# Eighteen chunks of softmax weights: computed on VectorE beside the attention, or left to ACT

## The chip, the cores and the metric

The kernel runs on one core of a Trainium2 chip. The metric is device time in microseconds (us) from the first to the last instruction of the core. Before the change it is 982.9 us, the median of three runs (981.16 to 983.02). The profile that is read below belongs to the run of 983.02 us; by its own records the span is 981.3 us, with a mean granted TensorE clock of 0.993 of full speed.

## The reference, cut to what matters

```python
# q: 4 x 12288 x 128, kv: 4 x 384 x 32 x 128, w_sr: 128 x 128
kv_pool = kv.reshape(B, H // 4, 4, W // 4, 4, C).mean(axis=(2, 4))   # 4 x 768 x 128
k = v = kv_pool.reshape(B, -1, C) @ w_sr
s = (q @ k.transpose(0, 2, 1)) / sqrt(128)
a = exp(s - max);  a /= a.sum(-1)
x = a @ v                                  # 49152 tokens x 128
h = x @ w_in                               # 49152 x 2048
g = h * sigmoid(1.702 * h)
out = g @ w_out                            # 49152 x 128
```

So there is an attention with 768 keys for each batch of queries, and behind it a feed-forward layer with a gate ("MoE" in the names, but with one expert).

## The kernel before

The tokens are cut into 96 groups of 512 (`NG`), four groups to a supergroup (24 of them, `NS`). The program runs twice through "attention, then feed-forward", each time for 12 supergroups. Within an attention the 768 keys of a group are six chunks of 128 keys (`JC`); a feed-forward has 16 chunks of 128 hidden features for each group.

A *fill* is a matmul with 512 columns into a bank of PSUM; three banks make a *unit*, and ACT turns a unit into weights with one instruction of 128x1536 (exponential in the attention, the gate function in the feed-forward). TensorE also works off the weights (*drain*): a feed-forward chunk with one matmul of 512 columns, an attention chunk with four matmuls of 129 columns, for which the text says "AV".

```python
def fill_attn(chunks, ps):
    for k, (i, jc) in enumerate(chunks):
        rhs = qTs[i // 4][:, 0, (i % 4) * G:(i % 4 + 1) * G]
        nc.tensor.matmul(ps[:, k, :], kTs[i // GB][:, jc * 128:(jc + 1) * 128], rhs,
                         start=True, stop=True)
    nc.scalar.activation(place([("a",) + c for c in chunks]), ps, AF.Exp, scale=scale)
```

`place` takes a free place in the ring `ag`, which has 102 places for chunks. A host loop at the end of the program decides in which order the instructions are emitted; it keeps a model of the time (`now` for TensorE in units of one matmul of 512 columns, `end` for ACT, `dve` for VectorE). The order on each engine is then fixed: an instruction that has to wait makes all later ones of its engine wait too.

```python
    FIXED, CHUNK, SWITCH, HANDOVER, EVACUATE, LATE = 0.295, 1.978, 6.0, 1.0, 4.5, 1.0
    ...
    SMALL, TURN = 0.26, 5.5
```

Some chunks of weights are made by VectorE instead of ACT. One matmul (line 391) fills a bank, and `early_exp` computes the exponential with ten instructions on 128x512:

```python
    def early_exp(ps, out):
        ...
        nc.vector.tensor_scalar(a, ps, scale / LN2, -126.0, MUL, MAX)
        nc.vector.tensor_scalar(b, a, 127.0, MAGIC, MIN, ADD)
        nc.vector.tensor_scalar(e, b, MAGIC - 127.0, 2.0 ** 23, SUB, MUL)
        nc.vector.scalar_tensor_tensor(b, b, MAGIC, a, SUB, SUB)
        nc.vector.tensor_scalar_mul(a, b, COEFFS[5])
        for k in (4, 3, 2, 1):
            nc.vector.scalar_tensor_tensor(a, a, COEFFS[k], b, ADD, MUL)
        nc.vector.scalar_tensor_tensor(out, a, COEFFS[0], e.bitcast(F32), ADD, MUL)
```

There are two kinds of them. Twenty-four (`early`: groups 48 to 51, all six chunks) are made during the first feed-forward, for the attention that follows. Eighteen (`rolling`) are made within the two attentions: the last chunk of the last group of a supergroup, for supergroups 5 to 11 and 13 to 23.

```python
    rolling = [(4 * s + 3, JC - 1) for s in range(NS) if 4 * s > early[-1] or QS < s < XS]
    aside = agpool.tile([128, K, 512], BF, name="aside")
    ...
    def early_fits(p, i, jc):
        if (i, jc) in rolling:
            group = ...                      # the group whose unit was filled last
            return (i // GB, jc) in vs and i // 4 - 1 <= group // 4 and len(used) > rolling.index((i, jc)) - K
        return low and min(slot_of.values()) >= low and (2, JC - 1) in vs

    def early_waits(t):                      # a tile's AV holds back until the model says the chunk is made
        return any(made.get((t // 4, jc), 1e9 if (t // 4, jc) in early_todo else 0.0) > now for jc in range(JC))
```

So the chunk of supergroup s is begun when the fills have come to supergroup s - 1. Its queries are in the tile `qT` of supergroup s, which is loaded by a transposing DMA that is issued two supergroups ahead:

```python
    def background(i):                       # called when group i is filled for the first time
        s = i // 4
        if i % 4 == 0:
            if QS <= s + 2 < NS:
                load_qT(s + 2)               # SyncE: transposing DMA from q_bf
            if CAST <= s + CAST < NS:
                gate()
                cast_q(s + CAST)             # GpSimd: q to bf16, DRAM to DRAM
        if i == 10:
            gate()
            for jc in range(JC):
                load_chunk(1, jc)            # GpSimd: keys of batch 1
```

Of the kernel before, what the change touches and what calls it, by code (L numbers as in the profile page):

```python
# [7 lines left out]
F32 = mybir.dt.float32  # L8
F32R = mybir.dt.float32r
I32 = mybir.dt.int32  # L10
BF = mybir.dt.bfloat16
# [13 lines left out]
def kernel(  # L25
    ctx, tc, q, kv, w_sr, moe_w_in, moe_w_out, out,
):
    nc = tc.nc
    B, N, C = q.shape
# [4 lines left out]
    JC = J // 128  # L34
# [5 lines left out]
    NG = B * N // G  # L40
    NS = NG // 4
    GB = NG // B
    SB = NS // B
    K = 3
    T = 128
    TS = 3
# [12 lines left out]
    R = 2  # L59
    XS = NS // R  # L60
# [3 lines left out]
    cpool = ctx.enter_context(tc.tile_pool(name="const", bufs=1))  # L64
# [5 lines left out]
    agpool = ctx.enter_context(tc.tile_pool(name="ag", bufs=1))  # L70
    npool = ctx.enter_context(tc.tile_pool(name="norm", bufs=3))
# [7 lines left out]
    banks = ppool.tile([128, 8, 512], F32, name="banks")  # L79
# [33 lines left out]
    kv_tiles, kv_sums, pooled, pTs, kTs, vs = {}, {}, {}, {}, {}, {}  # L113
# [32 lines left out]
    def value_chunk(b, jc):  # L146
        ps = acc()
        nc.tensor.matmul(ps[:, 0:128], pTs.pop((b, jc)), w_sr_sb, start=True, stop=True)
        nc.vector.tensor_copy(vs[b][:, jc, 0:C], ps[:, 0:128])
        vs[b, jc] = True  # L150

    def key_and_value(b, jc):
        if jc == 0:
            new_keys(b)
        ps = acc()
        nc.tensor.matmul(ps[:, 0:128], w_sr_sb, pTs[b, jc], start=True, stop=True)
        nc.tensor.matmul(ps[:, 128:256], pTs.pop((b, jc)), w_sr_sb, start=True, stop=True)
        nc.vector.tensor_copy(kTs[b][:, jc * 128:jc * 128 + 128], ps[:, 0:128])
        nc.vector.tensor_copy(vs[b][:, jc, 0:C], ps[:, 128:256])
        vs[b, jc] = True  # L160


    def add_kv(b, n):
# [26 lines left out]
    def make_v(b, a):  # L190
        ps = acc()
        pT = pTs.pop((b, a))
        for k in range(K):
            nc.tensor.matmul(ps[:, k * C:(k + 1) * C], pT[:, k * 128:(k + 1) * 128], w_sr_sb,
                             start=True, stop=True)
        nc.vector.tensor_copy(vs[b][:, a * K:(a + 1) * K, 0:C], ps[:, :h].rearrange("p (k c) -> p k c", k=K))
        for jc in range(a * K, a * K + K):
            vs[b, jc] = True

    qTs = {}  # L200

# [10 lines left out]
    QS = 4  # L212
# [19 lines left out]
        else:  # L232
            nc.vector.tensor_copy(dst, src)  # L233

    w_sr_f = npool.tile([128, 512], F32, name="ea", bufs=1)[:, 0:C]
    nc.sync.dma_start(out=w_sr_f, in_=w_sr)
    load_q(0, 0, 1)
    load_chunk(0, 0)
# [9 lines left out]
    ones = cpool.tile([128, 32], BF)  # L248
# [10 lines left out]
    for m in range(0, 128, 32):  # L259
        p = slice(m, m + 32)  # L260
# [17 lines left out]
    w_out_sb = cpool.tile([128, FCH, C], BF)  # L278

    ag = agpool.tile([128, AG, 512], BF, name="ag")  # L280
    wide = cpool.tile([128, 128], F32R)
    nc.vector.tensor_copy(wide.rearrange("p (a b) -> p a b", b=32), ones.unsqueeze(1).broadcast_to([128, 4, 32]))

    def warm_wide(n):
        for _ in range(n):
            nc.tensor.matmul(banks[:, 2, :], wide, wide.unsqueeze(1).broadcast_to([128, 4, 128]), start=True, stop=True)

    warm(8)
    transpose_q(0)
# [4 lines left out]
    slot_of = {}  # L294
    low = 0
# [26 lines left out]
        return K * len(free_frames())  # L322

    early = range(NG // R, NG // R + EARLY)
    rolling = [(4 * s + 3, JC - 1) for s in range(NS) if 4 * s > early[-1] or QS < s < XS]
    aside = agpool.tile([128, K, 512], BF, name="aside")

    def weights(c):
        if c[0] == "a" and c[1] in early:
            return ag[:, (c[1] - early[0]) * JC + c[2], :]  # L330
        if c[0] == "a" and c[1:] in rolling:
            return aside[:, rolling.index(c[1:]) % K, :]
        return ag[:, slot_of[c], :]


# [9 lines left out]
    def drain_attn(t, a):  # L345

        i, u, k = t // 4, t // TS, t % TS
        if k == a == 0:
            av_of[u] = acc(("av", u))
        o = t % 4 * T  # L350
        for jc in range(a * K, a * K + K):
            nc.tensor.matmul(av_of[u][:, k * (C + 1):(k + 1) * (C + 1)], weights(("a", i, jc))[:, o:o + T],  # L352
                             vs[i // GB][:, jc, 0:C + 1], start=(jc == 0), stop=(jc == JC - 1))
            if t % 4 == 3 and (i, jc) in rolling:
                used.append((i, jc))
            elif t % 4 == 3 and i not in early:
                del slot_of["a", i, jc]
        if k == TS - 1 and a == 1:
            close(("av", u), max(now, dve - 1.0) + EVACUATE)
            on_dve(4.3)  # L360
            ps = av_of.pop(u)[:, 0:TS * (C + 1)].rearrange("p (k c) -> p k c", k=TS)
            rec = npool.tile([128, TS], F32, name="rec")
            nc.vector.reciprocal(rec, ps[:, :, C])  # L363
            n, o = divmod(u * TS, RT)
            if o >= LATER[n]:
                to = x[:, o * T:(o + TS) * T].rearrange("p (k c) -> p k c", k=TS)
            else:
                if u % 2 == 0:
                    xt_of[u // 2] = npool.tile([128, 2 * TS, C], BF, name="xt")
                to = xt_of[u // 2][:, u % 2 * TS:u % 2 * TS + TS, :]  # L370
            nc.vector.tensor_tensor(to, ps[:, :, 0:C], rec.unsqueeze(2).broadcast_to([128, TS, C]), MUL)  # L371
            if u % 2 and o < LATER[n]:
                turns.append((now + TURN, u // 2))
            if n and (o + TS) % PART == 0:
                m = o // PART
                put_away(n, m)
                if m:
                    bring_back(n, m - 1)
                if m == RT // PART - 1:
                    bring_back(n, m)  # L380
# [14 lines left out]
    def early_step():  # L395
        nonlocal steps
        on_dve(next(steps))
        if steps.gi_frame.f_locals["last"]:
            steps = None
            made[early_todo.pop(0)] = dve  # L400

    def early_exp(ps, out):
        last = False
# [17 lines left out]
        last = True  # L421
        yield 3.5

    made, used = {}, []
    steps, early_todo = None, [c for c in rolling if c[0] < early[0]]
    early_todo += [(i, jc) for i in early for jc in range(JC)]
    early_todo += [c for c in rolling if c[0] > early[-1]]

    def early_fits(p, i, jc):
        if (i, jc) in rolling:  # L430
            group = seq[p][1][0][0] if seq[p][0] == "a" else seq[p][1][0][0] // (NG // R) * (NG // R) + NG // R - 1
            return (i // GB, jc) in vs and i // 4 - 1 <= group // 4 and len(used) > rolling.index((i, jc)) - K
        return low and min(slot_of.values()) >= low and (2, JC - 1) in vs

    def early_waits(t):
        return any(made.get((t // 4, jc), 1e9 if (t // 4, jc) in early_todo else 0.0) > now for jc in range(JC))

    def turn(w):

# [116 lines left out]
    chunks, sizes = [], [1, 3, 3, 1, 3, 1, 3, 1] + [3, 3, 2] * 4  # L556
    chunks += [(i, jc) for jc in range(2) for i in range(4)]
    chunks += [(i, jc) for jc in range(2) for i in range(4, 8)]
    chunks += [(i, jc) for jc in range(2, JC) for i in range(8)]
    chunks += [(i, jc) for i in range(8, NG) for jc in range(JC) if i not in early and (i, jc) not in rolling]  # L560
    seq, todo = [], []
    todo_early = [("a", t, a) for t in range(NT) for a in range(2) if (t // TS * TS + TS - 1) // 4 in early]
    for n in range(R):
# [12 lines left out]
    at = {}  # L576
# [3 lines left out]
    for i in early:  # L580
        for jc in range(JC):
            at["a", i, jc] = at["a", early[-1] + 1, 0] - 1
    for i, jc in rolling:
        at["a", i, jc] = at["a", i, 0]
    for kind, t, a in [k for k in todo + todo_early if k[0] == "a"]:
        at["at", t, a] = max(at["a", t // 4, jc] for jc in range(a * K, a * K + K))

# [46 lines left out]
    now, end, extra_at = 0.0, [], 0.0  # L634
    source, dve = None, 0.0
# [25 lines left out]
    for n in range(len(seq)):  # L661
        fill(n + 2)
        while True:
            room = room_ahead()
            limit = end[-1] - K - HANDOVER if n + 3 < len(seq) else 1e9
            bank = free[next_acc()]
            f = None
            if turns and max(now, bank) >= turns[0][0]:
                f, args = turn, turns[0][1:]
            if f is None and extras and now >= max(extra_at, bank):  # L670
                f, *args = extras[0]
            if steps and dve <= now + 2.0:
                early_step()
            if not f and not steps and early_todo and early_fits(min(n + 2, len(seq) - 1), *early_todo[0]) and dve <= now + 2.0 and now >= bank:
                f, args = early_fill, early_todo[0]
            if f and max(now, bank) + COST[f][0] > limit + (LATE if f is turn else 0.0 if f is early_fill else 4.5) and room >= 4 * K:
                f = None
            if f:
                now = max(now, bank) + COST[f][0]
# [11 lines left out]
                continue  # L691
            if not source:

                if todo_early and not any(early_waits(t) for t in range(todo_early[0][1], todo_early[0][1] + TS)):
                    source = todo_early
                else:
                    source = todo
            if not source:
                break
            kind, i, c = source[0]  # L700
            needs = at[("at" if kind == "a" else kind, i, c)]
            cost = K * SMALL if kind == "a" else 1.0
            first_of = c == 0 and (kind == "m" or i % TS == 0)
            if source is not todo_early and (needs > n or (kind == "a" and first_of and at["at", i + TS - 1, 1] > n)
                                             or (kind == "a" and (early_waits(i) or first_of and early_waits(i + TS - 1)))):
                if first_of:
                    source = None
                break
# [47 lines left out]
```

The softmax here doesn't subtract the row's maximum and nothing guards it: scores larger than these inputs give would overflow.

## Time and profile before

| engine | busy us | share of the span | what it does |
|---|---|---|---|
| PE (TensorE) | 953.1 | 97% | fills, drains, transposes |
| ACT | 936.9 | 95% | 512 gate units, 183 exponential instructions |
| DVE (VectorE) | 444.5 | 45% | 42 chunks of weights, evacuations, transposes of the output |
| POOL (GpSimd) | 65.7 | 7% | casting and accumulating DMAs |
| DMA | | mean 91 GB/s | 89.67 MB |

TensorE and ACT are both busy nearly all the time, so the places to look at are those where one of them is not. The page's second part gives the busy share of each engine in 40 slices of the span, 24.5 us each: in the third slice (49 to 74 us) PE and ACT both have the digit 6, between digits of 8 and 9, and the clock row has an 8. The order of the program: loads and first groups until about 40 us, first attention until 153 us, first feed-forward until about 505 us, second attention until 620 us, second feed-forward to the end.

### The profile page before, as it was taken

To read this page: it belongs to the slowest core of one execution; us is meant where nothing else is said; L and a number is where in the kernel's file an instruction comes from. 1 tells how busy PE (TensorE), PEld (TensorE's weight loads), DVE (VectorE), ACT (ScalarE), POOL (GpSimd) and SP (SyncE) were. 2 spreads that over 40 slices of the span, in tenths; PEclk is the share of its full clock that TensorE was granted. 3 is DMA by queue.
4 is the path that set the end of the run, shared out by engine and by line. 5 is a ranking of instruction groups with operands and counts; after the bars stand their busy time and mean duration, and the time that the engine had idled before them with its cause. 6 is when DMAs were issued, how large, how long until landed. Compare 5 with 4: busy or idle time off the path is not lost.

```text
span 981.3 us, 15454 instructions
## 1 busy us (share of the span) xinstructions
PE 953.1 (97%) x6359; PEld 508.6 (52%) x6359; DVE 444.5 (45%) x914; ACT 936.9 (95%) x700; POOL 65.7 (7%) x113
## 2 busy tenths in 40 slices
PE   7869999999999999999999999999999999999997
PEld 3546777744444444454445777664444444444443
DVE  4437767601477778777636677661101101101101
ACT  4969999999899999999999999999999999999995
POOL 3100100330000132000000000000000000000000
PEclk9989999999999999999999999999999999999999
DMA  9894752799772499324438776326222222222223
GB/s 182 164 194 87 118 99 45 108 150 172 160 141 33 77 150 137 45 33 77 64 57 137 162 140 147 91 65 125 37 43 42 34 43 42 36 42 43 34 42 53
DMA packets 354165, 89.67 MB, mean 91 GB/s; under 512 B 328048, under 2 KB 351728, under 8 KB 353776
## 3 DMA queue, kind: packets, MB, share of 16 engines
q1 hardware_dynamic: 323936, 56.06, 32.5%
q0 software_dynamic: 29104, 32.51, 21.7%
q8 instruction: 49, 0.80, 0.3%
q10 hardware_dynamic: 1056, 0.13, 0.1%
q14 instruction: 20, 0.16, 0.1%
HBM read 52.49 MB, written 45.88 MB: 100 GB/s over the span
## 4 chain that ended last, share of the span: by engine, by line
PE 82%; ACT 13%; DMA 3%; DVE 1%; issue 0%; POOL 0%; POOLq 0%
PE banks L540 34%; PE banks L533 32%; ACT ag L343 9%; PE banks L352 7%; PE banks L341 7%; ACT ag L535 3%; DMA qT<-q_bf 2%; PE banks L391 1%; DMA x<-in_q_dram 1%; DVE qT L233 1%; PE banks L444 0%; DVE xt L371 0%; PE banks L227 0%; PE banks L134 0%; DVE x L446 0%
## 5 line engine op out<-in xcount | busy, mean ns | idle before, releaser
L535 ACT ACTIVATE ag<-banks 128x1536 bf16<-128x1536 f32 x512 | 689.6, 1519 | 6.4 <-PE banks L533 6.2
L533 PE MATMUL banks<-x,w_in_sb 128*128 128x512 bf16 x1536 | 415.0, 379 | 4.0 <-ACT ag L535 3.0
L540 PE MATMUL banks<-ag,w_out_sb 128*128 128x512 bf16 x1536 | 410.2, 379 | 0.0
L343 ACT ACTIVATE ag<-banks 128x1536 bf16<-128x1536 f32 (+1 forms) x183 | 241.5, 1496 | 22.0 <-PE banks L341 21.9
L540 PEld LDWEIGHTS <-w_out_sb 128*128 128x128 bf16 x1536 | 149.9, 98 | 179.2 <-issue 0.2
L533 PEld LDWEIGHTS <-w_in_sb 128*128 128x128 bf16 x1536 | 147.9, 98 | 172.8 <-issue 6.9
L548 DVE STREAM_TRANSPOSE o_sb<-banks 128x512 f32<-128x512 f32 x96 | 68.8, 716 | 360.0 <-PE banks L540 344.3
L352 PEld LDWEIGHTS <-ag 128*128 128x128 bf16 x2232 | 145.6, 98 | 45.7 <-issue 1.0
L352 PE MATMUL banks<-v,ag 128*128 128x129 bf16 x2232 | 164.1, 221 | 0.4 <-DVE xt L371 0.2
L341 PE MATMUL banks<-qT,kT 128*128 128x512 bf16 x534 | 146.5, 382 | 5.6 <-ACT ag L343 4.5
L418 DVE SCALAR_TENSOR_TENSOR ea<-ea,eb 128x512 f32<-128x512 f32 x168 | 115.2, 686 | 3.8
L341 PEld LDWEIGHTS <-kT 128*128 128x128 bf16 x534 | 47.0, 98 | 35.4 <-issue 5.1
L371 DVE TENSOR_TENSOR x<-banks,rec 128x384 bf16<-128x384 f32 x104 | 58.0, 558 | 3.6
L407 DVE TENSOR_SCALAR ea<-banks 128x512 f32<-128x512 f32 x42 | 29.1, 692 | 60.1 <-PE banks L391 59.9
L363 DVE RECIPROCAL rec<-banks 128x3 f32<-128x3 f32 x128 | 22.9, 179 | 55.2 <-PE banks L352 54.9
L168 POOL DMA_DIRECT2D kvs<-in_kv_dram x32 | 40.5, 1299 | 33.5 <-DMA kvs<-in_kv_dram 31.1
L469 POOL MEMSET gate_tile<- 1x8 f32 x38 | 3.9, 101 | 450.8 <-DVE gate_tile L468 450.7
L413 DVE SCALAR_TENSOR_TENSOR eb<-eb,ea 128x512 f32<-128x512 f32 x42 | 28.9, 689 | 1.0
L391 PE MATMUL banks<-qT,kT 128*128 128x512 bf16 x42 | 16.1, 384 | 9.1 <-DMA qT<-q_bf 9.1
L415 DVE TENSOR_SCALAR ea<-eb 128x512 f32<-128x512 f32 x42 | 18.2, 434 | 0.9
L411 DVE TENSOR_SCALAR ee<-eb 128x512 int32<-128x512 f32 x42 | 17.9, 427 | 1.3
L409 DVE TENSOR_SCALAR eb<-ea 128x512 f32<-128x512 f32 x42 | 17.8, 423 | 1.0
(68 smaller groups left out, 199.9 us busy)
## 6 DMA issues: line engine op xcount, KB each, us to landing
out_dram<-o_sb SPq DMA_DIRECT2D x382, 64.0 KB, 2.0
kvs<-in_kv_dram POOLq DMA_DIRECT2D x32, 384.0 KB, 6.5
q_bf<-in_q_dram POOLq DMA_DIRECT2D x20, 512.0 KB, 5.8
x_bf<-x SPq DMA_DIRECT2D x13, 768.0 KB, 5.7
x<-in_kv_dram POOLq DMA_DIRECT2D x12, 512.0 KB, 12.4
x<-in_q_dram POOLq DMA_DIRECT2D x3, 512.0 KB, 20.2
w_in_sb<-in_moe_w_in_dram POOLq DMA_DIRECT2D x1, 512.0 KB, 5.2
w_out_sb<-in_moe_w_out_dram POOLq DMA_DIRECT2D x1, 512.0 KB, 6.6
```

Source lines behind the costliest of these rows:

```text
L168: nc.gpsimd.dma_start(out=kv_sums[b][:, i2], in_=kv_p[b, i, w, :, i2], **({"accum_op": ADD} if n else {}))
L341: nc.tensor.matmul(ps[:, k, :], kTs[i // GB][:, jc * 128:(jc + 1) * 128], rhs, start=True, stop=True)
L343: nc.scalar.activation(place([("a",) + c for c in chunks]), ps, AF.Exp, scale=scale)
L352: nc.tensor.matmul(av_of[u][:, k * (C + 1):(k + 1) * (C + 1)], weights(("a", i, jc))[:, o:o + T], vs[i // GB][:, jc, 0:C + 1], start=(jc = ...
L371: nc.vector.tensor_tensor(to, ps[:, :, 0:C], rec.unsqueeze(2).broadcast_to([128, TS, C]), MUL)
L407: nc.vector.tensor_scalar(a, ps, scale / LN2, -126.0, MUL, MAX)
L413: nc.vector.scalar_tensor_tensor(b, b, MAGIC, a, SUB, SUB)
L418: nc.vector.scalar_tensor_tensor(a, a, COEFFS[k], b, ADD, MUL)
L533: nc.tensor.matmul(ps[:, k, :], w_in_sb[:, fc * 128:(fc + 1) * 128], x[:, g % (4 * XS) * G:(g % (4 * XS) + 1) * G], start=True, stop=True)
L535: nc.scalar.activation(place([("m",) + c for c in chunks]), ps, AF.Gelu_apprx_sigmoid)
L540: nc.tensor.matmul(o_of[g], w_out_sb[:, fc, :], weights(("m", g, fc)), start=(fc == 0), stop=(fc == FCH - 1))
L548: nc.vector.transpose(o_sb, o_of.pop(g))
```

## The change

The eighteen chunks go back to ACT. They are taken out of VectorE's list, come back into ACT's sequence of units, and take places in the ring `ag` as all others do; the tile `aside` goes. The twenty-four early chunks of the first feed-forward stay on VectorE. The stated lengths of TensorE's small jobs and of ACT's units (the constants above) are the same in both versions. The purpose: the attention no longer needs VectorE to deliver weights in time.

```diff
-    rolling = [(4 * s + 3, JC - 1) for s in range(NS) if 4 * s > early[-1] or QS < s < XS]
-    aside = agpool.tile([128, K, 512], BF, name="aside")
 
     def weights(c):
         if c[0] == "a" and c[1] in early:
             return ag[:, (c[1] - early[0]) * JC + c[2], :]
-        if c[0] == "a" and c[1:] in rolling:
-            return aside[:, rolling.index(c[1:]) % K, :]
         return ag[:, slot_of[c], :]
...
-    made, used = {}, []
-    steps, early_todo = None, [c for c in rolling if c[0] < early[0]]
-    early_todo += [(i, jc) for i in early for jc in range(JC)]
-    early_todo += [c for c in rolling if c[0] > early[-1]]
...                                    (early_fits and early_waits go)
+    made = set()
+    steps, early_todo = None, [(i, jc) for i in early for jc in range(JC)]
...
-    chunks += [(i, jc) for i in range(8, NG) for jc in range(JC) if i not in early and (i, jc) not in rolling]
+    chunks += [(i, jc) for i in range(8, NG) for jc in range(JC) if i not in early]
...                                    (emitting loop)
-            if not f and not steps and early_todo and early_fits(min(n + 2, len(seq) - 1), *early_todo[0]) and dve <= now + 2.0 and now >= bank:
+            if not f and not steps and early_todo and low and min(slot_of.values()) >= low and (2, 1) in vs and dve <= now + 2.0 and now >= bank:
                 f, args = early_fill, early_todo[0]
...
-                                             or (kind == "a" and (early_waits(i) or first_of and early_waits(i + TS - 1)))):
+                                             or (kind == "a" and i // 4 in early and (i // 4, JC - 1) not in made)):
```

Two small parts come along. The operand of four warming matmuls at the start is written out at 128x512, where it was 128x128 and read four times over; and `w_sr` is loaded into a tile of its own instead of one that VectorE uses later.

```diff
-    w_sr_f = npool.tile([128, 512], F32, name="ea", bufs=1)[:, 0:C]
+    w_sr_f = cpool.tile([128, C], F32)
...
-    wide = cpool.tile([128, 128], F32R)
-    nc.vector.tensor_copy(wide.rearrange("p (a b) -> p a b", b=32), ones.unsqueeze(1).broadcast_to([128, 4, 32]))
+    wide = cpool.tile([128, 16, 32], F32R)
+    nc.vector.tensor_copy(wide, ones.unsqueeze(1).broadcast_to([128, 16, 32]))
```

More of the change, by code (lines that the diff above doesn't have):

```diff
@@ L149, in value_chunk @@
         nc.vector.tensor_copy(vs[b][:, jc, 0:C], ps[:, 0:128])
-        vs[b, jc] = True
     def key_and_value(b, jc):
@@ L159, in key_and_value @@
         nc.vector.tensor_copy(vs[b][:, jc, 0:C], ps[:, 128:256])
-        vs[b, jc] = True
     def add_kv(b, n):
@@ L196, in make_v @@
         nc.vector.tensor_copy(vs[b][:, a * K:(a + 1) * K, 0:C], ps[:, :h].rearrange("p (k c) -> p k c", k=K))
-        for jc in range(a * K, a * K + K):
-            vs[b, jc] = True
+        vs[b, a] = True
     qTs = {}
@@ L280 @@
     ag = agpool.tile([128, AG, 512], BF, name="ag")
-    wide = cpool.tile([128, 128], F32R)
-    nc.vector.tensor_copy(wide.rearrange("p (a b) -> p a b", b=32), ones.unsqueeze(1).broadcast_to([128, 4, 32]))
+    wide = cpool.tile([128, 16, 32], F32R)
+    nc.vector.tensor_copy(wide, ones.unsqueeze(1).broadcast_to([128, 16, 32]))
     def warm_wide(n):
         for _ in range(n):
-            nc.tensor.matmul(banks[:, 2, :], wide, wide.unsqueeze(1).broadcast_to([128, 4, 128]), start=True, stop=True)
+            nc.tensor.matmul(banks[:, 2, :], wide[:, 0:4, :].rearrange("p a b -> p (a b)"), wide, start=True, stop=True)
     warm(8)
@@ L353, in drain_attn @@
                              vs[i // GB][:, jc, 0:C + 1], start=(jc == 0), stop=(jc == JC - 1))
-            if t % 4 == 3 and (i, jc) in rolling:
-                used.append((i, jc))
-            elif t % 4 == 3 and i not in early:
+            if t % 4 == 3 and i not in early:
                 del slot_of["a", i, jc]
@@ L399, in early_step @@
             steps = None
-            made[early_todo.pop(0)] = dve
+            made.add(early_todo.pop(0))
     def early_exp(ps, out):
@@ L422, in early_exp @@
         yield 3.5
-    made, used = {}, []
-    steps, early_todo = None, [c for c in rolling if c[0] < early[0]]
-    early_todo += [(i, jc) for i in early for jc in range(JC)]
-    early_todo += [c for c in rolling if c[0] > early[-1]]
[L429 to L436, printed above, removed]
+    made = set()
+    steps, early_todo = None, [(i, jc) for i in early for jc in range(JC)]
     def turn(w):
@@ L582 @@
             at["a", i, jc] = at["a", early[-1] + 1, 0] - 1
-    for i, jc in rolling:
-        at["a", i, jc] = at["a", i, 0]
     for kind, t, a in [k for k in todo + todo_early if k[0] == "a"]:
@@ L692 @@
             if not source:
-                if todo_early and not any(early_waits(t) for t in range(todo_early[0][1], todo_early[0][1] + TS)):
+                if todo_early and all((i, jc) in made for t in range(todo_early[0][1], todo_early[0][1] + TS)
+                                      for i in [t // 4] for jc in range(JC)):
                     source = todo_early
```

## The prediction

> **What bounds the kernel now.** I read the page's groups first, then rates from the timeline near the end, then the waits of 55 to 80 us and the timeline of that hole, then stretches of 20 us. The groups give busy time, mean length in ns, and the idle time before with its releaser:
>
> ```profile
> L535 ACT ACTIVATE ag<-banks 128x1536 bf16<-128x1536 f32 x512 | 689.6, 1519 | 6.4 <-PE banks L533 6.2
> ...
> L343 ACT ACTIVATE ag<-banks 128x1536 bf16<-128x1536 f32 (+1 forms) x183 | 241.5, 1496 | 22.0 <-PE banks L341 21.9
> ...
> L391 PE MATMUL banks<-qT,kT 128*128 128x512 bf16 x42 | 16.1, 384 | 9.1 <-DMA qT<-q_bf 9.1
> ```
>
> The reader is to see that ACT is busy 931 of 981 us and that the one large wait of TensorE is for queries, before line 391, the fill for VectorE. Instructions overlap, so what one costs is read from runs of them (start, length, count):
>
> ```profile
> 954.21 14.93 ACT L535 ACTIVATE ag<-banks 128x1536 bf16<-128x1536 f32 x11
> ...
> 967.45 8.58 PE L540 MATMUL banks<-ag,w_out_sb 128*128 128x512 bf16 x39
> ```
>
> An ACT unit costs (14.93 - 1.52) / 10 = 1.34 us, 0.447 us a chunk; a 512-column matmul (8.58 - 0.38) / 38 = 0.216 us. A feed-forward unit needs six matmuls, 1.29 us of TensorE, against 1.34 of ACT: ACT is the slower engine by 0.05 us a unit, and TensorE has that much to work off arrears. At the end TensorE has 39 drains left when ACT is nearly done.
>
> The hole (waits of 55 to 80 us, then the timeline):
>
> ```profile
> ACT ag L343 <- PE banks L341: 11.4, 3, 9.8
> ...
> PE banks L391 <- DMA qT<-q_bf: 9.1, 1, 9.1
> ```
>
> ```profile
> 61.30 0.56 PE L134 MATMUL banks<-sum,x 128*128 128x32 bf16 x16
> ...
> 70.97 0.61 PE L391 MATMUL banks<-qT,kT 128*128 128x512 bf16 x1 [9.11 <-DMA qT<-q_bf]
> ...
> 71.37 1.49 PE L341 MATMUL banks<-qT,kT 128*128 128x512 bf16 x3
> ```
>
> The first rolling chunk (supergroup 5) stands in TensorE's queue at 62 us; its queries land at 70.9 us, 22.9 us after the issue at 48.06 us. Everything behind it waits, ACT for 11.4 us. Stretches (length, busy us of PE, PEld, DVE, ACT, POOL with counts, granted clock, DMA):
>
> ```profile
> 60.00:80.00 20.00, 10.89 (x104) 7.26 (x103) 7.79 (x21) 8.59 (x7) 0.00 (x0) 0.74 0.67 124
> ...
> 600.00:620.00 20.00, 19.95 (x216) 14.12 (x214) 13.64 (x32) 20.00 (x16) 0.00 (x0) 1.00 0.46 107
> 620.00:640.00 20.00, 18.38 (x205) 13.09 (x202) 14.36 (x32) 19.82 (x16) 0.00 (x0) 1.00 0.35 81
> 640.00:660.00 20.00, 18.01 (x175) 11.66 (x173) 14.05 (x30) 20.00 (x16) 0.00 (x0) 1.00 0.36 79
> ...
> 700.00:720.00 20.00, 20.00 (x94) 9.11 (x93) 2.15 (x3) 20.00 (x16) 0.00 (x0) 1.00 0.26 40
> ```
>
> There are two places where TensorE isn't full: 60 to 80 us, and 620 to 660 us, where AV waits for the last three rolling chunks, each begun 13 to 15 us after the one before (line 391 at 618.6, 634.1, 647.6 us), and the feed-forward's drains stand behind AV.
>
> **What the Trainium skill says.** "TensorE: Matmul & The Clock Gate", section "Wait — 56ns, not 53.3ns?", gives 215.7 ns start to start for 512 columns at full clock; the trace agrees with 216 ns. The same page, "What's actually happening", says that an idle window of about 3.4 us halves the clock and about as much activity restores it; the trace shows 0.51 granted from 71 to 77 us, after the hole. "DMA: Bandwidth & Descriptors", section "Queues, rings and completion order", says that each DMA engine takes turns between queues a packet at a time. That fits the slow load: it shares the engines with six loads of keys and the casts of q, with packets of 4 KB and 32 KB against its own of 256 B.
>
> **The change part by part.**
>
> 1. VectorE loses 18 chunks of ten instructions: 0.692 + 0.423 + 0.427 + 0.689 + 0.434 + 4 x 0.686 + 0.681 = 6.09 us each, 110 us in all. It is at 45%; by itself this gives nothing.
>
> 2. ACT gets 18 chunks, six units: 18 x 0.447 = +8.05 us. Seven fall into the first attention (+3.1), eleven into the second (+4.9). Both have ACT at 20.00 of 20 us, so all of it lies on the path. TensorE's matmuls are the same in number; 18 move from line 391 to line 341.
>
> 3. The hole at 62 us. Up to there order and DMAs are the same in both. Without the rolling chunk the queries of supergroup 5 are first needed by the fill of group 20. Group 16 is first filled at 59.38 us (its gate is at 58.93), and eight units later is 59.4 + 8 x 1.34 = 70.1 us. They land at 70.9: TensorE waits 0.8 us, ACT perhaps 0.5. ACT gains 11.4 - 0.5 = 10.9 us. The next load is done at about 73 us in the trace and is needed at about 81, so no new hole should come behind.
>
> 4. TensorE's arrears. In the first attention it lost 9.1 us in the hole and about half of the 6 us at half clock, 12 us; the attention becomes shorter by 10.9 - 3.1 = 7.8 us, so it gains 4 us on ACT. Between 620 and 660 us it gets back the 20.00 - 18.38 + 20.00 - 18.01 = 3.6 us, and the second attention's extra 4.9 us of ACT are time in which it drains. 4 + 3.6 + 4.9 = 12.5 us, more than the 8.4 us of arrears at the end. The last drains should then follow ACT directly, about 2 us where it was (967.45 + 8.58) - (954.21 + 14.93) = 6.9.
>
> 5. With shorter arrears, some of ACT's 6.2 us of waiting for line 533 goes; I take 1.5 us (a choice; the rest comes where key and value jobs are pushed in).
>
> 6. The longer cast for the warming matmuls is one VectorE instruction at 5.4 us, 0.29 us now and perhaps four times that (an estimate from the width); TensorE then waits for keys until 7.09 us anyway. I count 0 to 0.3 us.
>
> Sum by ACT: it ends at 969.1 now; 969.1 - 10.9 + 8.05 - 1.5 = 964.8 us. Plus 2 us of drains, plus 5.2 us from TensorE's end (976.0) to the end of the span (981.3) for the last transpose and stores: 972 us. The measured time is 1.6 us above the span: 973.6 us, 0.9% faster.
>
> **The rivals.**
>
> A. The wait only changes its place: the fill of group 20 meets the same late load, or a later load becomes late because the program now comes to it 10 us earlier. For it: the margin is 0.8 us on the wrong side. Against it: landing time and need come from the same undisturbed stretch of trace. If the hole came back whole, the time would be 982.9 + 8.05 - 5 (less arrears at the end) = 986 us; if half of it came back, 979 us.
>
> B. TensorE is the bound, and ACT's 8 us vanish in its shadow: the gain would be what TensorE gets back, 12 + 3.6 = 15.6 us, 967 us. For it: PE busy 953 us. Against it: in the steady stretch it needs 1.29 us of 1.34 a unit, and the busy share of pipelined matmuls overstates it.
>
> C. VectorE's help was worth its 8 us and the hole isn't due to it: 991 us. Against it: the instruction that waits is line 391 itself, and it is emitted for a rolling chunk.
>
> **Range and chances.** From A by half (979) and a little, to B (967): 967 to 981 us. Faster by 2% would need less than 963.2 us; ACT alone would end at about 960 us, with 7 us behind it, even if all its waiting for line 533 went, so 4%. Slower by 2% needs 1002 us, which no rival reaches: 1%.
>
> **What would show it.** In the profile after: line 391 occurs 24 times, line 341 552 times; ACT's exponentials take about 8 us more. From 60 to 80 us both engines are full and the clock stays at 1.00; a wait for queries of at most 1 us stands before line 341. From 620 to 660 us (some us earlier) TensorE has no holes. The run of line 540 at the end is some 10 instead of 39. It would be wrong if a wait for a load of queries of several us appeared before line 341, or if ACT's idle time in the feed-forwards grew.

## The result, and the profile after

The changed kernel takes 968.9 us (median of four runs, 968.77 to 969.1) against 982.6 us for the kernel before (now the median of four): a ratio of 0.9863, with an interval of 0.9846 to 0.9880. That is 13.7 us, where 9 were predicted. The span of the profiled execution falls from 981.3 to 967.3 us.

The line numbers have moved: 334 is the fill of the attention (341 before), 382 the fill for VectorE (391), 336 and 515 are ACT's instructions (343 and 535), 513 and 520 the feed-forward's fills and drains (533 and 540). The groups of the profile after, with busy time, mean in ns, and idle time before with its releasers:

```profile
L515 ACT ACTIVATE ag<-banks 128x1536 bf16<-128x1536 f32 x512 | 688.9, 1539 | 1.2 <-PE banks L513 1.0
...
L336 ACT ACTIVATE ag<-banks 128x1536 bf16<-128x1536 f32 (+1 forms) x188 | 249.9, 1456 | 12.1 <-PE banks L334 12.0
...
L382 PE MATMUL banks<-qT,kT 128*128 128x512 bf16 x24 | 9.1, 379 | 0.0
```

ACT's exponentials cost 8.4 us more, as they had to (241.5 before). But its idle time falls on both lines: from 22.0 to 12.1 us before the exponentials, and from 6.4 to 1.2 us before the gate units. Line 382 occurs 24 times, and TensorE no longer waits in front of it.

The place of the hole, in the timeline after, and then the stretches of 20 us (busy us of PE, PEld, DVE, ACT, POOL with counts; granted clock; DMA share and GB/s):

```profile
69.98 0.50 PE L345 MATMUL banks<-v,ag 128*128 128x129 bf16 x6
71.91 0.82 PE L334 MATMUL banks<-qT,kT 128*128 128x512 bf16 x3 [1.43 <-DMA qT<-q_bf]
```

```profile
60.00:80.00 20.00, 18.53 (x250) 13.35 (x249) 9.37 (x31) 18.49 (x15) 0.58 (x2) 1.00 1.00 177
...
620.00:640.00 20.00, 20.00 (x199) 13.42 (x197) 6.62 (x18) 20.00 (x16) 0.00 (x0) 1.00 0.50 111
640.00:660.00 20.00, 20.00 (x94) 9.07 (x93) 2.15 (x3) 20.00 (x16) 0.00 (x0) 1.00 0.68 127
...
920.00:940.00 20.00, 20.00 (x91) 8.62 (x90) 2.15 (x3) 20.00 (x16) 0.00 (x0) 1.00 0.26 40
```

A wait of 1.4 us for queries stands where one of 9.1 us stood, and the clock stays full. From 620 to 660 us TensorE is busy throughout. In the last stretch it runs 91 matmuls where 94 fit (700 to 720 us before): it has caught up with ACT and waits for it, which the busy share doesn't show, because its matmuls overlap (379 ns each, 216 ns from start to start). So does the end, TensorE's last lines:

```profile
958.80 0.81 PE L513 MATMUL banks<-x,w_in_sb 128*128 128x512 bf16 x3
959.45 1.51 PE L520 MATMUL banks<-ag,w_out_sb 128*128 128x512 bf16 x6
961.49 0.81 PE L520 MATMUL banks<-ag,w_out_sb 128*128 128x512 bf16 x3 [0.53 <-ACT ag L515]
```

Nine drains behind the last fill instead of 39, the last three waiting for ACT's last unit.

To see where a time comes from, all runs below are cut at the end of ACT's last unit of each stage. "Tail" is from ACT's last unit to the end of the span. The numbers are worked out from the traces' start and length of ACT's instructions:

| kernel | rolling chunks, by supergroup | attention 1 ends | feed-forward 1 | attention 2 | feed-forward 2 | tail | span | measured |
|---|---|---|---|---|---|---|---|---|
| before | 5-11, 13-23 | 155.7 | 351.8 | 114.8 | 346.8 | 12.1 | 981.3 | 982.6 |
| changed | none | 148.6 | 347.3 | 120.1 | 345.5 | 5.9 | 967.3 | 968.9 |
| e4_only_s5 | 5 | 157.7 | 348.0 | 120.1 | 345.5 | 5.9 | 977.1 | 978.9 |
| e1_without_s5 | 6-11, 13-23 | 146.2 | 352.4 | 114.8 | 346.8 | 12.1 | 972.2 | 974.1 |
| e5_s5_later | as before, 5 begun later | 145.6 | 352.0 | 114.8 | 346.9 | 12.1 | 971.4 | 972.9 |
| e2_first_only | 6-11 | 146.4 | 352.4 | 120.0 | 345.5 | 5.9 | 970.2 | 972.6 |
| e3_second_only | 13-23 | 148.5 | 346.3 | 114.8 | 346.9 | 12.1 | 968.6 | 970.4 |
| e6_none | none, the rest as before | 148.6 | 346.3 | 120.1 | 345.5 | 5.9 | 966.3 | 968.2 |
| e8_small_ring | none, ring of 90 | 149.0 | 349.3 | 120.1 | 345.5 | 5.9 | 969.8 | 971.4 |
| e9_late_low | 6-11, ring cut later | 146.4 | 350.5 | 120.0 | 345.7 | 5.9 | 968.5 | 970.7 |
| e7_alternate_second | 14, 16, 18, 20, 22 | 148.7 | 346.3 | 119.8 | 346.0 | 5.9 | 966.7 | 968.8 |
| e10_alternate_later | the same, begun later | 148.5 | 346.3 | 117.8 | 346.0 | 5.9 | 964.4 | 966.4 |
| e11_seven_later | 13, 14, 16, 17, 19, 20, 22, begun later | 149.1 | 346.3 | 116.7 | 345.7 | 6.0 | 963.8 | 965.6 |

Before and after, stage by stage: -7.1, -4.5, +5.3, -1.3, -6.2, in all -13.8 us (-13.9 unrounded).

### The profile page after: what moved, and what is told of

Read it like the earlier page. It is cut to its first block, busy times and chain, and to the rows that moved or that the text cites. A ratio compares the mean times of both kernels' runs of the same rounds, so it can differ in the third digit from the quotient of the medians.

```text
span 967.3 us, 15236 instructions
## 1 busy us (share of the span) xinstructions
PE 950.7 (98%) x6359; PEld 505.5 (52%) x6359; DVE 345.2 (36%) x734; ACT 944.5 (98%) x705; POOL 65.7 (7%) x113
## 4 chain that ended last, share of the span: by engine, by line
PE 50%; ACT 45%; DMA 3%; DVE 1%; issue 0%; POOL 0%; ACTq 0%; POOLq 0%
ACT ag L515 36%; PE banks L520 17%; PE banks L513 17%; ACT ag L336 9%; PE banks L345 7%; PE banks L334 7%; DMA qT<-q_bf 2%; DMA x<-in_q_dram 1%; DVE qT L230 1%; PE banks L382 1%; PE banks L224 0%; PE banks L424 0%; DVE o_sb L528 0%; ACT L515 0%; PE banks L134 0%
## 5 line engine op out<-in xcount | busy, mean ns | idle before, releaser
L336 ACT ACTIVATE ag<-banks 128x1536 bf16<-128x1536 f32 (+1 forms) x188 | 249.9, 1456 | 12.1 <-PE banks L334 12.0
L334 PE MATMUL banks<-qT,kT 128*128 128x512 bf16 x552 | 149.7, 379 | 6.9 <-ACT ag L336 4.5
L409 DVE SCALAR_TENSOR_TENSOR ea<-ea,eb 128x512 f32<-128x512 f32 x96 | 66.0, 687 | 2.8
L398 DVE TENSOR_SCALAR ea<-banks 128x512 f32<-128x512 f32 x24 | 16.6, 692 | 28.8 <-PE banks L382 28.8
L411 DVE SCALAR_TENSOR_TENSOR ag<-ea,ee 128x512 bf16<-128x512 f32 x24 | 16.6, 690 | 0.8
L404 DVE SCALAR_TENSOR_TENSOR eb<-eb,ea 128x512 f32<-128x512 f32 x24 | 16.4, 683 | 0.6
L362 DVE TENSOR_TENSOR xt<-banks,rec 128x384 bf16<-128x384 f32 x24 | 13.4, 558 | 0.8
L230 DVE COPY qT<-banks 128x512 bf16<-128x512 bf16 x15 | 9.8, 688 | 4.6 <-PE banks L224 4.5
L426 DVE COPY x<-banks 128x768 bf16<-128x768 bf16 x12 | 6.7, 558 | 12.8 <-PE banks L424 12.8
```

## The experiments

Except for e8, all are edits of the kernel before, mostly of its list of rolling chunks. Theory 1 was that the time went into two places where work waits for VectorE's chunks (the hole at 62 us and the end of the second attention) and that the rest is ACT's arithmetic; theory 2 had other culprits in each case.

**e4_only_s5: the hole alone.**

```diff
-    rolling = [(4 * s + 3, JC - 1) for s in range(NS) if 4 * s > early[-1] or QS < s < XS]
+    rolling = [(4 * s + 3, JC - 1) for s in [5]]
```

> One rolling chunk alone, that of supergroup 5; the other 17 are made by ACT as after the change. Theory 1 (the load of queries makes a hole, and the hole leaves TensorE in arrears for which ACT waits later): TensorE waits some 9 us before the fill for VectorE at about 62 us, ACT waits again for fills in the first feed-forward (4 to 5 us in all), and the time is 976 to 982 us, that is 8 to 13 us above the 968.9 us of the changed kernel. Theory 2 (it is the eighteen deliveries by VectorE that cost, each a little, because AV waits for them): one chunk costs under 1 us, 968 to 970 us.

Measured: 978.9 us, 0.9969 of the kernel before (0.9957 to 0.9982). One chunk out of eighteen costs 10 of the 13.7 us. The waits of its trace from 55 to 80 us (us in total, times, longest):

```profile
ACT ag L343 <- PE banks L341: 10.6, 2, 9.6
...
PE banks L391 <- DMA qT<-q_bf: 8.9, 1, 8.9
```

The same wait as in the kernel before, on the same load. The second half of theory 1 failed: the first feed-forward is only 0.7 us longer than in the changed kernel (1.6 us longer than in e6 below, which differs from e4 by this chunk alone), ACT waits 1.6 us for fills there, not 4 to 5, and the tail is as short. The arrears of TensorE that the hole leaves are not what ACT waited for later.

**e1_without_s5 and e5_s5_later: the hole taken away in two ways.** e1 leaves the chunk of supergroup 5 to ACT. e5 keeps all 18 and begins this one four groups later:

```diff
-            return (i // GB, jc) in vs and i // 4 - 1 <= group // 4 and ...
+            return (i // GB, jc) in vs and i // 4 - 1 <= group // 4 and (i > 23 or group >= 20) and ...
```

> The kernel before with 17 rolling chunks, all but that of supergroup 5. Theory 1: no hole at 62 us; ACT has 17 x 0.43 = 7.3 us less than in the changed kernel, but AV still waits for VectorE behind the second attention (3 to 6 us of TensorE), so the run ends with TensorE in arrears: 964 to 969 us. Theory 2: most of the loss stays: 976 to 982 us.

> The kernel before with all 18 chunks, where only the chunk of supergroup 5 is begun four groups later, when group 20 is filled, by which time its queries are there. Theory 1 (the hole is a matter of when the chunk is begun, not of the chunk): the time is that of the kernel without this chunk, 974.1 us, within 1 us. Theory 2 (the chunk itself, VectorE's work or the shared tile, costs it): 980 us or more.

Measured: e1 974.1 us (0.9920, 0.9905 to 0.9935), e5 972.9 us (0.9905, 0.9889 to 0.9922). They end the first attention 9.5 and 10.1 us earlier than before. So the hole is a matter of when the fill for VectorE stands in TensorE's queue, not of VectorE doing this chunk. That e5 is 1.2 us better than e1 was a little outside what was expected and isn't explained. But both are slower than the changed kernel, where I had expected 964 to 969 us for e1: the other chunks cost 4 to 5 us too.

**e2_first_only and e3_second_only: the other seventeen, by attention.** Their lists are `range(6, 12)` and `range(13, 24)`.

> Six rolling chunks, supergroups 6 to 11, none in the second attention. Theory 1: no hole, no wait of AV behind the second attention, ACT 6 x 0.43 = 2.6 us shorter than in the changed kernel: 966 to 967 us. Theory 2: a third of the loss, 971 to 974 us.

> Eleven rolling chunks, supergroups 13 to 23, none in the first attention. Theory 1: ACT 4.7 us shorter than in the changed kernel, but AV behind the second attention waits for VectorE and TensorE loses 4 to 6 us there, so that TensorE has 20 or more drains left when ACT ends: 966 to 969 us. Theory 2: two thirds of the loss, 975 to 979 us.

Measured: e2 972.6 us (0.9904, 0.9889 to 0.9919), e3 970.4 us (0.9882, 0.9867 to 0.9897). e2 lies in theory 2's range, e3 between the two. The table says what happened. The six chunks of the first attention save ACT 2.2 us there, and the first feed-forward gets 5.1 us longer (6.0 against e6, the right partner, so that this half of the program ends 3.9 us later with them than without). The eleven of the second save 5.3 us there, and come back as 1.4 us in the second feed-forward and 6.2 us in the tail.

For the eleven, the profile shows the mechanism that was predicted. VectorE's first and last instruction of its last chunks in e3, on the timeline (ACT ends the attention at 610 us), and then TensorE's last line:

```profile
606.31 0.69 DVE L407 TENSOR_SCALAR ea<-banks 128x512 f32<-128x512 f32 x1 [1.59 <-PE banks L391]
...
619.22 0.68 DVE L420 SCALAR_TENSOR_TENSOR aside<-ea,ee 128x512 bf16<-128x512 f32 x1
...
620.89 0.69 DVE L407 TENSOR_SCALAR ea<-banks 128x512 f32<-128x512 f32 x1 [0.99 <-PE banks L391]
...
632.20 0.68 DVE L420 SCALAR_TENSOR_TENSOR aside<-ea,ee 128x512 bf16<-128x512 f32 x1
...
635.32 0.69 DVE L407 TENSOR_SCALAR ea<-banks 128x512 f32<-128x512 f32 x1 [2.44 <-PE banks L391]
```

```profile
954.77 8.58 PE L540 MATMUL banks<-ag,w_out_sb 128*128 128x512 bf16 x39
```

A chunk takes 14 to 15 us here, while ACT needs 23 x 0.447 = 10.3 us for the other chunks of a supergroup. VectorE falls further behind with each, its last chunks are begun when the attention's fills are over, AV waits, and the 39 drains are back at the end. VectorE isn't full while it falls behind: it is busy 14.7 of 20 us (600 to 620 us), and before each of these chunks it waits 1.0 to 2.4 us for the fill. So it is slow in the order in which this program gives it work; whether another order would let it keep up with eleven chunks was not tried. (About 2% of the matmul records are missing in the traces of e1 to e4, so TensorE's gaps are not read from them.)

**e6_none: the side parts.** The list is empty; the rest is the kernel before.

> The kernel before with an empty list of rolling chunks: what then still differs from the changed kernel is only the side parts (the operand of the warming matmuls at 128x128, the shared tile of w_sr) and the finer test for when AV may start on the 24 early chunks. If these are worth nothing, 968.5 to 969.3 us, the time of the changed kernel; a time of 971 or more would mean that part of the gain comes from them.

Measured: 968.2 us (0.9859, 0.9843 to 0.9876), 0.3 us under the expected range. The wider operand, the tile for `w_sr` and the coarser test for the early chunks bring nothing to the gain; the first feed-forward is 0.9 us shorter without them. The changed kernel would be better off with the finer test, if it is that; which of the three it is was not tried.

**e8_small_ring and e9_late_low: what the six chunks come back as.** In e2, ACT's waits in the first feed-forward (from 150 to 500 us) are those of the kernel before (5.2 us in 6 waits):

```profile
ACT ag L535 <- PE banks L533: 5.3, 7, 1.4
```

and the timeline of e2 shows TensorE late with fills because it drains in long runs first:

```profile
251.46 0.81 PE L533 MATMUL banks<-x,w_in_sb 128*128 128x512 bf16 x3
252.11 2.32 PE L540 MATMUL banks<-ag,w_out_sb 128*128 128x512 bf16 x10
254.26 0.81 PE L533 MATMUL banks<-x,w_in_sb 128*128 128x512 bf16 x3
254.91 1.46 PE L540 MATMUL banks<-ag,w_out_sb 128*128 128x512 bf16 x6
```

Either the ring is full, so that drains must come first, or the small jobs for keys and values push in. e8 takes twelve places from the ring of the changed kernel; e9 is e2 with the 24 places for early chunks cut out of the ring three groups later.

```diff
 # e8, from the changed kernel
-    AG = 102
+    AG = 90
 # e9, from e2
-        if g == 12:
+        if g == 15:
             low = EARLY * JC
```

> The changed kernel with 90 places in the ring in place of 102. Theory 1 (the six chunks of the first attention come back as ACT's waits in the first feed-forward because weights that TensorE has not drained yet fill the ring): twelve places less have the same effect as twelve chunks more of arrears, ACT waits 3 to 6 us more in the first feed-forward, 971 to 975 us. Theory 2 (the ring has room to spare and the waits come from the small jobs for keys and values): no change, 968.5 to 969.5 us.

> Six rolling chunks in the first attention (the kernel of 972.6 us), but the 24 places for the early chunks are taken out of the ring three groups later (from group 15 of the first feed-forward on, not 12), some 21 us in which TensorE can work off arrears at 0.05 us a unit. Theory 1 (room in the ring): ACT's 5.6 us of waits in the first feed-forward shrink by 1 to 3 us, 969.5 to 971.5 us. Theory 2 (small jobs): no change, 972 to 973 us.

Measured: e8 971.4 us (0.9888, 0.9874 to 0.9903), e9 970.7 us (0.9881, 0.9867 to 0.9896). ACT's waits for fills in the first feed-forward of e8, against 1.0 us in the changed kernel:

```profile
ACT ag L515 <- PE banks L513: 2.5, 5, 1.1
```

and in e9, against e2's 5.3 (the times are as theory 1 had them; e8's waits grew by 1.5 us, where 3 to 6 were expected):

```profile
ACT ag L535 <- PE banks L533: 3.6, 6, 1.1
```

Less room makes the waits and more room takes a third of them away, so the ring has a part in them. The number of feed-forward chunks that are filled and not yet drained, counted from the starts of the matmuls, shows how. In the kernel before it is 82 at the 180th fill, shortly before the ring is cut (group 12, chunk 192), and 69 at the 240th: TensorE has had to drain, and ACT waits 1.2 and 1.4 us at 260 and 265 us. In e9, with the later cut, it is still 82 at the 240th, and a wait of 1.1 us comes at 286 us. In the changed kernel and in e6 it is 58 both times, and there is no wait of this kind.

Near the end of the stage all three of the kernels below stand at the limit. Up to the last fill of the first feed-forward, the kernel before has run lines 533 and 540 this often, the changed kernel lines 513 and 520, and e8 the same two lines (stretch, its length, busy us and count):

```profile
0.00:505.43 505.43, 207.14 (x767) 0.99 0.69 111
...
0.00:505.43 505.43, 189.63 (x701) 0.99 0.69 111
```

```profile
0.00:493.81 493.81, 207.14 (x767) 1.00 0.71 113
...
0.00:493.81 493.81, 189.42 (x700) 1.00 0.71 113
```

```profile
0.00:496.24 496.24, 207.13 (x767) 1.00 0.71 113
...
0.00:496.24 496.24, 192.71 (x713) 1.00 0.71 113
```

Chunks that are filled and not yet drained: 66 before, 67 after, 54 in e8. The 24 early places are still cut out, so 102 - 24 = 78 are left, and 66 in e8: all three stand some twelve places under their limit. That is a number of the emitting loop, with K = 3:

```python
            if start + cost > limit and not (room < 2 * K + 1 or (room < 4 * K and start == now)):
                ...                          # no drain now: the next fill goes first
```

With fewer than twelve places free, a drain that can start at once is emitted even if it makes the next fill late. The first half of the program therefore ends when TensorE says so, whatever ACT saved in the attention.

Not settled: a full ring can take back the 2.2 us that ACT saved, but e2 and e9 end the first feed-forward 3.9 and 2.0 us later than e6. In e9 TensorE itself loses time. Counted from start to start beyond a matmul's usual interval (216 ns for 512 columns, 57 ns for those of 128 and 129), it loses 2.5 us between 80 and 210 us, and in e6 nothing. The waits with a named cause are 0.7 us of it, all for VectorE. So these chunks also cost TensorE time, by a way that isn't shown. The other 1.9 us of e2 go away with e9's later cut; why TensorE, which sets the end, loses them is open.

**e7, e10 and e11: can some of VectorE's help be kept?** If VectorE is too slow for one chunk a supergroup, one in two should do (e7: `range(14, 24, 2)`).

> Five rolling chunks, every other supergroup of the second attention (14 to 22). Theory 1 (VectorE is too slow at one chunk a supergroup: 14.8 us a chunk in the trace of the eleven, against 10.2 us in which ACT makes the other 23): at one in two supergroups it keeps up, AV does not wait behind the attention, ACT saves 5 x 0.44 = 2.2 us and the run ends 5.9 us behind ACT as in the changed kernel: 966 to 967.5 us. Theory 2 (TensorE has no time left, so that whatever ACT saves in the second attention comes back at the end): 968.5 to 970 us.

Measured: 968.8 us (0.9861, 0.9847 to 0.9876), no gain on e6's 968.2. The tail stayed short, but the second attention is only 0.2 us shorter than in e6. The timeline of TensorE has the reason:

```profile
559.26 0.33 PE L352 MATMUL banks<-v,ag 128*128 128x129 bf16 x3
561.43 0.39 PE L391 MATMUL banks<-qT,kT 128*128 128x512 bf16 x1 [1.84 <-DMA qT<-q_bf]
```

The hole of 62 us again, small: the fill for VectorE comes a supergroup earlier than ACT's fill would, and the load of its queries isn't done. On SyncE's queue it had stood behind the loads of the feed-forward's input:

```profile
546.31 9.67 SPq L461 DMA_TRANSPOSE x<-x_bf  x1
556.09 5.13 SPq L209 DMA_TRANSPOSE qT<-q_bf  x2
```

So e10 begins each chunk two groups later, and e11 does so with seven chunks:

```diff
-            return (i // GB, jc) in vs and i // 4 - 1 <= group // 4 and ...
+            return (i // GB, jc) in vs and i - 5 <= group and ...
```

> Five rolling chunks in the second attention as in the kernel of 968.8 us, but each begun two groups later in its supergroup's lead (from group 4s - 2 on, not 4s - 4), so that its queries have 5 us longer to land. Theory 1 (there the 2.2 us that ACT saves went into one wait of 1.8 us for queries, the same fault as at 62 us in the kernel before): the wait goes and the saving stays, 966 to 967 us against 968.2 us with none. Theory 2 (TensorE's time is the bound and gives nothing back): 968 to 969 us.

> Seven rolling chunks (supergroups 13, 14, 16, 17, 19, 20, 22), begun as late as in the five. ACT saves 3.1 us; TensorE has about 4.4 us left at the end of the kernel with none, so if VectorE keeps up (two chunks in three supergroups, 29.6 of 31.5 us by the rate of the eleven) 965 to 966.5 us by theory 1; if VectorE falls behind, AV waits and it is 967 to 969 us.

Measured: e10 966.4 us (0.9838, 0.9824 to 0.9853), e11 965.6 us (0.9826, 0.9810 to 0.9842; four runs from 965.29 to 965.78). e11 is 3.3 us under the changed kernel by the medians and 2.6 us under e6, its partner without rolling chunks; they were timed in different sets of runs, each against the kernel before, and the intervals of the ratios just fail to touch (e11 ends at 0.9842, e6 begins at 0.9843, the changed kernel at 0.9846). In e11 TensorE ends so:

```profile
955.37 0.81 PE L533 MATMUL banks<-x,w_in_sb 128*128 128x512 bf16 x3
956.01 2.75 PE L540 MATMUL banks<-ag,w_out_sb 128*128 128x512 bf16 x12
```

Twelve drains without a wait: TensorE and ACT now end together, and there is little left to move from one to the other.

## Why the prediction was right, point by point

The measured 968.9 us lies within 967 to 981, near its lower end, and is 4.7 us under the predicted 973.6: the gain was half as large again as the 9 us forecast. The spans compare the same way, 967.3 with 972.0.

1. VectorE's loss of work costs nothing: right. The lengths of its instructions fall by 109 us in sum, for 110 predicted, its busy time by 99 us (444.5 to 345.2; they overlap a little), and no stage suffers for it.
2. ACT's six units: predicted +8.05 us. It stands in the sum of its busy time (936.9 to 944.5) as +7.6. In the second attention all of it is on the path, +5.3 of the stage for +4.9 predicted.
3. The hole: predicted 10.9 us back for ACT, with 0.5 of 11.4 left. Measured 9.9: the wait for the same load became 1.4 us on TensorE and 1.5 us on ACT, because the load landed at 71.9 us, 1 us later than before, and the fill was wanted at 70.5; I had allowed at most 1 us. No other load became late. e4 and e5 show that this hole, and its place in the queue, is what it was taken for.
4. The arrears at the end: right in kind, and e3 shows the cause, AV behind VectorE. But of the three terms in the sum, 4 + 3.6 + 4.9, the first had no part in it: e4 keeps the hole and has the short tail of 5.9 us, e5 loses the hole and keeps the long one of 12.1 us. What the hole costs is all there at the end of the first feed-forward (505.6 us in e4, 494.9 in e6). The other two terms, 8.5 us, just cover the 8.4 us of arrears, so the conclusion stood in spite of this step. The tail lost 6.2 us where 4.9 were counted; TensorE's last matmul ends 0.9 us behind ACT, not 2.
5. ACT's waits for line 533: this is the term that was mis-sized. I took 1.5 us of 6.2 and put the rest down to key and value jobs. They fell by 5.2 us. The runs show where they came from: the six chunks put ACT ahead of TensorE in the first attention (e2 has the waits without the hole, e6 has 0.4 us of them without the chunks), and the ring was then too full of undrained weights to hide it (e8 makes waits with a smaller ring, e9 takes a part away with a later cut). How much of the lead is TensorE's own lost time is the open end above. The rest of the difference is in points 2 to 4.
6. The side parts: predicted 0 to 0.3 us for the warming operand. Its cast takes 0.50 us, not four times 0.29. e6 says that all that isn't the list costs about 0.7 us, in the first feed-forward and not at the start.

Of the rivals, A (the wait only changes its place) is out; its shadow was the 1.4 us. B (TensorE is the bound) came nearer with its 967 us than I did with 973.6. It is right up to the end of the first feed-forward, where the ring ties ACT to TensorE; the last fill there comes 11.6 us earlier, about what the hole gave TensorE: 9.1 less the 1.4 us that are left, and half of the 6 us at half clock, 10.7 us. From the second attention on the sum by ACT holds: in the page's chain of work that ended last, ACT's line 515 has 36% of the span, where line 535 had 3% before. C (VectorE's help was worth 8 us) was wrong for a reason it didn't have: in the first attention its help cost 4.5 us even without the hole (e2 against e6), and in the second it came too slowly (e3, 2.3 us worse than e6); seven chunks in place of eleven, begun later, are worth 2.6 us (e11 against e6).

## What to carry to other kernels

An in-order queue turns an early request for a late load into a stop of everything behind it: when work is brought forward to another engine, check not only that the engine has time, but when its inputs land. Work taken off one of two balanced engines gains only until the buffer between them is full, so ask for each stage who sets its end, and look for the saving as a wait one stage later. And a helper engine must keep the pace of the stage that it helps, by its own measured time per piece in that stage; if it doesn't, giving it less can make the whole faster.

## What the runs showed of the hardware that had not been expected

VectorE's ten instructions for a chunk take 6.1 us by their lengths. From first to last they took 6.9 us beside the feed-forward (507 to 514 us, before), but 10.7 to 12.3 us in the middle of the second attention, beside AV's evacuations, with a chunk in every other supergroup (539.7 to 550.4 us in e7, 523.1 to 535.2 us in e10) and 11 to 13.6 us with one in each (606.3 to 619.9 us in e3), with VectorE busy 14.4 of 20 us in the same place before (620 to 640 us). The instructions keep their lengths; the gaps lie between them, where evacuations and waits for AV were put.

A wait of 1.4 us left TensorE's granted clock at 1.00 (60 to 80 us, after), while the wait of 9.1 us was followed by 0.51 (71 to 77 us, before). By the trace's clock records the half clock there lasts from 66.7 to 76.9 us: it begins 4.8 us after TensorE has stopped and ends 6.0 us after it is at work again, which is more than the prediction's "about as much activity" as the 3.4 us of idling.
